# Gate scans in two pieces, and real products in the pauses before the first MLP pair, in an mLSTM and Fourier-mixing kernel

## The chip, the cores and the metric

The kernel runs on one core of one Trainium2 chip. A core has five engines that run at the same time and meet only at semaphores: TensorE (PE; the loading of its stationary operand is listed as PEld), VectorE (DVE), ScalarE (ACT), GpSimd (POOL) and SyncE (SP), which here issues the transfers. The metric is device time of one execution in microseconds (us); smaller is better.

## What is computed

Four sequences (batches) of 768 tokens pass through eight mLSTM heads of width 40, and the result, 320 wide, passes through a Fourier mix and an MLP. All is float32. Cut to what matters:

```python
# mLSTM, per batch, head and step t
m_new  = maximum(f_gate[t] + m, i_gate[t])
f_stab = exp(f_gate[t] + m - m_new);  i_stab = exp(i_gate[t] - m_new)
C = f_stab * C + i_stab * outer(v[t], k[t]);  n = f_stab * n + i_stab * k[t]
y[t] = sigmoid(o_gate[t]) * (C @ q[t]) / maximum(abs(n @ q[t]), 1)
# Fourier mix and MLP; x is (4, 768, 320), w_ch1 (320, 1280), w_ch2 (1280, 320)
u  = x + real(fft(fft(x, axis=seq), axis=feature))
un = (u - mean(u)) / sqrt(var(u) + 1e-6)
out = u + maximum(un @ w_ch1, 0) @ w_ch2
```

## The kernel before

The tokens are cut into six chunks of 128 (`NT = 6`, `L = 128`). Inside a chunk the recurrence is a masked product of scores and weights; between chunks a state `C` is carried. The running maximum `m` is a scan over tokens; all 32 (batch, head) rows are scanned at once in 32 partitions. Batches and chunks are counted from 0 below.

Every piece of work is entered in a plan by slot and phase, and the plan is emitted in order. Each engine then takes its own instructions strictly in the order in which they were emitted:

```python
EVAC, FILL, MAIN, FILL_PE = range(4)          # phases within a slot
def at(slot, phase, fn, *args): plan.setdefault((slot, phase), []).append((fn, args))
```

The gates come first. `sums` scans f within each chunk (F), `maxima` scans the running maximum M, `weights` makes wk = exp(a - M_last) on ACT, `decay` makes g on ACT, `columns` transposes rows to columns on PE. `parts` splits M into three bf16 parts on POOL, so that `spread_max` can spread a row of M over all partitions with a bf16 product; chunk 0 alone is spread in float32 from M itself, with a column of the identity:

```python
def spread_max(b, c, h0):
    ...
    k.M.append(bank("pM", [L, NP, L]))
    nc.tensor.matmul(k.M[-1], ident_b, later_b..., start=True, stop=False, ...)        # the mask
    for h in range(h0, h0 + NP):
        bh = b * H + h
        w, x = (ident[:, bh:bh + 1], M[:, c, :]) if c == 0 else (sel[:, bh:bh + 1], M3[:, c, :])
        nc.tensor.matmul(k.M[-1][:, h - h0, :], w.to_broadcast([w.shape[0], L]), x, ...)

first, second, others = slice(0, 1), slice(1, 2), slice(2, NT)
sums(first); maxima(first, M_INIT)
pt = columns(first, 0); nc.scalar.copy(out=colT[:, first, 0], in_=pt[:, first])
weights(first)
spread_max(0, 0, 0)
pt = columns(first, 1)
sums(second); maxima(second, M[0:BH, 0, L - 1:L]); parts(second)
columns_out(first, 1, pt)
pt = columns(second, 0)
spread_max(0, 0, NP)
mlstm_scores(0, 0); mlstm_exp(0, 0, 0); mlstm_exp(0, 0, NP)
mlstm_load_o(0, 1)
columns_out(second, 0, pt)
nc.vector.memset(g[:, 1:3], 0.0)
sums(others); maxima(others, M[0:BH, 1, L - 1:L])
decay(second); weights(second)
spread_max(0, 1, 0); spread_max(0, 1, NP); spread_decay(0, 1)
late = {1: columns(second, 1), 0: columns(others, 0)}
...
at(1, FILL + 0.2, parts, others)
at(2, FILL + 0.5, columns_late)            # DVE copies of late[1] and late[0]
at(4, FILL - 0.4, decay_late)              # g of the others (ACT), stored to G_d (SP)
at(5, FILL + 0.3, weights, others)         # wk of chunks 2 to 5 (ACT)
at(5, FILL_PE + 1.8, columns_last)         # their transposes (PE)
at(6, FILL - 0.2, ...)                     # and their copy to colT (DVE)
at(5, FILL_PE + 2.1, spread_decay, 0, 2)
for c in range(2, NT):
    for h0 in (0, NP): at(3 * c - 1, FILL_PE + 2, spread_max, 0, c, h0)
```

The plan of the mLSTM, for chunk c of batch b in slot s = s0 + 3 c (s0 is 0, 32, 50, 82 for the four batches), cut:

```python
if b > 0:
    t = 22 + 2 * c if b == 1 and c < 3 else s - 5
    at(t, FILL, mlstm_load, b, c); at(t, FILL, mlstm_load_max, b, c); at(t, FILL, mlstm_load_decay, b, c)
...
at(s - 1 if last else s, FILL_PE + (2.05 if last else 2), mlstm_scores, b, c)    # PE: k times q
at(s + 2, FILL, mlstm_weigh, b, c)          # DVE: scores times weights
at(s + 3, FILL_PE, mlstm_from_state, b, c)  # PE: C times q
at(s + 3, FILL_PE + 3, mlstm_from_chunk, b, c); at(s + 3, FILL_PE + 3, mlstm_to_state, b, c)
at(s + 4, FILL, mlstm_gather, b, c)         # ACT: out of PSUM, the state among it
```

(The first chunk of the first batch and the last one are placed apart.) The weights of the MLP come as 64-bit floats in ten pieces of 640 KB (`raw`) and are turned into float32 by DVE (`take`: L358, L360; `join`: L372, L374, L378) and ACT (`convert`: L365, L366), with two buffers for `raw`.

Where the first mix ends and the MLP begins (slots 22 to 31), PE has a few products of zeros in its plan, in slots 24, 25 and 26, each of 256 columns:

```python
def idle_products(n, first=False):
    pw = bank("pi", ...) if first else ps_s.tile([L, 2 * L], FP, name="pi", tag="ps")
    for i in range(n): nc.tensor.matmul(pw, rest[:, 0:L], rest, ...)
```

`mix_add` (DVE) adds the mix to x and takes the mean and variance of a chunk of tokens, `mix_center` (ACT) centers it, `mix_turn` (PE) transposes it, `mix_turn_out` (ACT) copies it to `uT`. The MLP of batch 0 takes three chunks of tokens at a time (a group; 384 columns), and two blocks of 128 hidden features at a time (a pair):

```python
def mlp_in(b, gr, f):
    if f % 2 == 0: k.pm = [bank("pm", [L, TG * L]) for _ in range(2)]
    for i, ch in ((1, 1),) if f % 2 else ((0, 0), (0, 1), (1, 0)):
        nc.tensor.matmul(k.pm[i], w1_sb[:, ch, ...], u[2 * ch], start=(ch == 0), stop=False)
    if f % 2:
        for i in range(2): nc.tensor.matmul(k.pm[i], w1t_sb[r, ...], u[1][r], start=False, stop=True)
```

PSUM has four banks for such use; the string `turn` says which bank each new tile takes.

Of the kernel before, what the change touches and what calls it, by code (L numbers as in the profile page):

```python
# [10 lines left out]
FP = mybir.dt.float32  # L11
# [8 lines left out]
L = 128  # L20
# [30 lines left out]
def kernel(  # L51
# [28 lines left out]
    ps_h = pool("ps_h", 2, space=PSUM)  # L80
    ps_m = pool("ps_m", 1, space=PSUM)

    turn = iter("3210321032120312031230123012012301023130201320132013201320123021320321")

    def bank(name, shape, n=None):

        return ps_m.tile(shape, FP, name=name, tag=f"pm{next(turn) if n is None else n}")
# [43 lines left out]
    EVAC, FILL, MAIN, FILL_PE = range(4)  # L131


    def idle_products(n, first=False):
        pw = bank("pi", [L, 2 * L]) if first else ps_s.tile([L, 2 * L], FP, name="pi", tag="ps")
        for i in range(n):
            nc.tensor.matmul(pw, rest[:, 0:L], rest, start=True, stop=True, skip_group_check=True)


    def gates(gp):  # L140
# [19 lines left out]
        idle_products(3, True)  # L160
        mlstm_load(0, 0)
        make_identity(nc, ident)
        nc.gpsimd.memset(later_b, 0.0)
# [5 lines left out]
        nc.vector.memset(keep, 1.0)  # L169
        nc.vector.memset(keep[:, :, 0:1], 0.0)  # L170
        nc.vector.memset(shift, 0.0)
        nc.vector.memset(M[:, 0:1], 0.0)
        for t in C_bufs:
            nc.scalar.copy(out=t.rearrange("p (two n) t -> p two (n t)", two=2),
                           in_=rest.unsqueeze(1).to_broadcast([L, 2, 2 * L]))
# [30 lines left out]
        def spread_max(b, c, h0):  # L206

            k = chunks[b, c]
            if h0 == 0:
                k.W = wp.tile([L, H, L], FP, name="W", tag="W")  # L210
                k.M = []
            k.M.append(bank("pM", [L, NP, L]))
            nc.tensor.matmul(k.M[-1], ident_b, later_b.unsqueeze(1).to_broadcast([L, NP, L]), start=True, stop=False,
                             skip_group_check=True)
            for h in range(h0, h0 + NP):
                bh = b * H + h
                w, x = (ident[:, bh:bh + 1], M[:, c, :]) if c == 0 else (sel[:, bh:bh + 1], M3[:, c, :])
# [31 lines left out]
                nc.tensor.transpose(pt[:, c, :], (a, wk)[j][:, c, :], ident[0:BH, 0:BH])  # L249
            return pt  # L250


        first, second, others = slice(0, 1), slice(1, 2), slice(2, NT)

        def columns_out(s, j, pt):
            nc.vector.tensor_copy(out=colT[:, s, j], in_=pt[:, s])

        sums(first)
        maxima(first, M_INIT)
        pt = columns(first, 0)  # L260
# [1 line left out]
        weights(first)  # L262
        spread_max(0, 0, 0)
        pt = columns(first, 1)
        sums(second)
        maxima(second, M[0:BH, 0, L - 1:L])
        parts(second)
        columns_out(first, 1, pt)
        pt = columns(second, 0)
        spread_max(0, 0, NP)  # L270
        mlstm_scores(0, 0)
        mlstm_exp(0, 0, 0)
        mlstm_exp(0, 0, NP)
        mlstm_load_o(0, 1)
        columns_out(second, 0, pt)
        nc.vector.memset(g[:, 1:3], 0.0)
        sums(others)
        maxima(others, M[0:BH, 1, L - 1:L])
        decay(second)
        weights(second)  # L280
        spread_max(0, 1, 0)
        spread_max(0, 1, NP)
        spread_decay(0, 1)
        late = {1: columns(second, 1), 0: columns(others, 0)}

        def clear(*tiles):
            for t in tiles:
                nc.gpsimd.memset(t, 0.0)

        def columns_late():  # L290
            columns_out(second, 1, late[1])
            columns_out(others, 0, late[0])

        def columns_last():
            late[2] = columns(others, 1)

        def decay_late():
            decay(others)
            for hip in range(2):
                nc.sync.dma_start(out=G_d[1:NT, hip].rearrange("c p t -> p c t"), in_=g[hip:BH:2, 1:NT])  # L300

# [13 lines left out]
            nc.sync.dma_start(out=M_d.rearrange("c p t -> p c t"), in_=M[0:BH])  # L315

        at(12, FILL + 0.7, maxima_out)
        at(1, FILL + 0.2, parts, others)
        at(5, FILL + 0.3, weights, others)
        at(5, FILL_PE + 1.8, columns_last)  # L320
        at(6, FILL - 0.2, lambda: columns_out(others, 1, late[2]))
        at(5, FILL_PE + 2.1, spread_decay, 0, 2)
        for c in range(2, NT):
            for h0 in (0, NP):
# [147 lines left out]
    def mlstm_scores(b, c):  # L472

        k = chunks[b, c]
        k.ps = [ps_s.tile([L, NP, L], FP, name=f"ps{hip}", tag="ps") for hip in range(2)]
        for p in range(NP):
            for hip in range(2):
                r = slice(hip * 64, hip * 64 + D)
                nc.tensor.matmul(k.ps[hip][:, p, :], k.qk[r, 1, p, :], k.qk[r, 0, p, :], start=True, stop=True)  # L479
# [87 lines left out]
    def plan_mlstm(b, s0, stride=3):  # L567
        for c in range(NT):
            s = s0 + stride * c
            if b > 0:  # L570
                t = 22 + 2 * c if b == 1 and c < 3 else s - 5
                at(t, FILL, mlstm_load, b, c)
                at(t, FILL, mlstm_load_max, b, c)
                at(t, FILL, mlstm_load_decay, b, c)
                at(s, FILL, mlstm_load_o, b, c)
            if (b, c) > (0, 0):
                at(s, FILL, mlstm_exp, b, c, 0)
                at(s + 1, FILL - 0.5, mlstm_exp, b, c, NP)
                last = (b, c) == (0, NT - 1)
                at(s - 1 if last else s, FILL_PE + (2.05 if last else 2), mlstm_scores, b, c)  # L580
                if b > 0:
                    at(s + 1, FILL, mlstm_mask, b, c)
            at(s, FILL, mlstm_scale_v, b, c)
            at(s if (b, c) == (0, 2) else s + 1, FILL + 0.1, mlstm_scale_q, b, c)
            at(s + 2, FILL, mlstm_decay, b, c)
            end = (b, c) == (0, NT - 1)
            at(s + 1 if end else s + 2, FILL - 0.4 if end else FILL, mlstm_weigh, b, c)
            at(s + 2 if end else s + 3, FILL_PE, mlstm_from_state, b, c)
            at(s + 2 if end else s + 3, FILL_PE + (2 if end else 3), mlstm_from_chunk, b, c)
            at(s + 3, FILL_PE + 3, mlstm_to_state, b, c)  # L590
            at(s + 3 if end else s + 4, FILL, mlstm_gather, b, c)
            if b == 0:
                t, x = ((8, 11), (11, 14), (13, 14), (14, 15.5), (17, 18), (18, 21))[c]
            else:
                t = s + (8, 8, 7, 5, 5, 5)[c]
                x = t + 1
            at(t, FILL_PE + ((2.5 if c < 4 else 1) if b == 0 else 1), mlstm_turn, b, c, b == 0 and c < 4)
            at(x, FILL + 0.05, mlstm_finish, b, c)
# [240 lines left out]
                at(t + 1, EVAC, mix_turn_out, b, c)  # L839


    def mlp_in(b, gr, f):


        k = mixes[b]
        u = [uT_bufs[gr][:, ch].rearrange("p c t -> p (c t)") for ch in range(3)]
        if f % 2 == 0:
            k.pm = [bank("pm", [L, TG * L]) for _ in range(2)]
        for i, ch in ((1, 1),) if f % 2 else ((0, 0), (0, 1), (1, 0)):
            f0 = (f // 2 * 2 + i) * L  # L850
            nc.tensor.matmul(k.pm[i], w1_sb[:, ch, f0:f0 + L], u[2 * ch], start=(ch == 0), stop=False)  # L851
        if f % 2:
            for i in range(2):
                r = slice(i * TAIL, (i + 1) * TAIL)
                nc.tensor.matmul(k.pm[i], w1t_sb[r, f // 2 * L:(f // 2 + 1) * L], u[1][r], start=False, stop=True)  # L855


    hid = {}
# [185 lines left out]
    def plan_mlp(b, s):  # L1044
# [7 lines left out]
                at(*((s, EVAC) if end else (s + n, MAIN + 0.5)), mlp_relu_in_place, gr, f)  # L1052
        for gr in groups if b == 0 else ():
            for f in range(NFF):
                at(s, MAIN, mlp_in, b, gr, f)
                s += 1
                if f % 2:
                    at(s, EVAC, mlp_relu, b, gr, f - 1)
                    at(s, EVAC, mlp_relu, b, gr, f)
# [24 lines left out]
    def plan_batch(b, s_mlstm, s_mix, s_mlp):  # L1084
# [161 lines left out]
```

## Time and profile before

| What | Value |
|---|---|
| time, median of 3 runs | 428.91 us (427.86 to 429.19) |
| span of the profiled execution | 427.5 us |
| mean granted PE clock, share of full speed | 0.984 |
| read from and written to device memory | 42.52 MB and 4.11 MB |
| `sums`, 128 and 512 columns (L191) | 0.41 and 1.15 us |
| scan of M, 128 and 512 columns (L199) | 0.47 and 1.27 us |
| one half of `spread_max`, float32, full clock (L213 and L218) | 0.39 and 1.09 us |
| one half of `spread_max`, bf16, full clock (L213 and L218) | 0.39 and 0.39 us |
| first `pu` product of the mix (L743) | starts at 58.85 us |

A line of the timeline gives start, length, engine, source line (L), operation, what is written and what is read, and in square brackets how long the engine had been idle before it and whom it waited for. A line of a group of waits gives engine, line and tile, then the one waited for, the total, the number of times and the longest. Float32 products appear as two matmul records each. Ends of matmuls are modelled, since PE works pipelined.

### The profile page before, as it was taken

The numbers are of one execution on the slowest core, as the hardware profiler recorded it, in microseconds if no ns is written. First come the engines' busy times: TensorE is split into PE (matmuls) and PEld (weight loads), VectorE is DVE, ScalarE is ACT, GpSimd is POOL, SyncE is SP. The second block draws the span as 40 slices with busy tenths as digits, with TensorE's granted clock in tenths as the row PEclk, the third lists the DMA queues.
The fourth block names the chain that finished last, engine by engine and source line by source line (L and its number), as shares of the span: only waits on it lengthen the run. The fifth ranks groups of instructions, "written<-read, shape, count | busy, mean of one in ns | idle before, by whom it ended". The sixth has DMA issues, their size and how long they took to land.

```text
span 427.5 us, 7999 instructions
## 1 busy us (share of the span) xinstructions
PE 412.9 (97%) x2958; PEld 305.4 (71%) x2958; DVE 289.0 (68%) x690; ACT 189.3 (44%) x493; POOL 116.8 (27%) x199
## 2 busy tenths in 40 slices
PE   8699899999999999999999999999999999999997
PEld 6478645566667777777557999977558988555996
DVE  7558886857997736687766487797754586335552
ACT  7637646767544411455546414464452023345000
POOL 7615501238642440433051152333030000020000
PEclk9669999999999999999999999999999999999999
DMA  7846849567763441546400343420000000000010
GB/s 233 272 138 166 301 124 283 191 215 208 224 200 115 159 145 44 158 144 189 141 0 1 95 151 117 139 65 2 0 2 0 32 31 18 15 0 2 15 45 33
DMA packets 20549, 47.14 MB, mean 110 GB/s; under 512 B 2784, under 2 KB 9312, under 8 KB 20384
## 3 DMA queue, kind: packets, MB, share of 16 engines
q1 hardware_dynamic: 20512, 46.65, 34.8%
q8 instruction: 23, 0.38, 0.4%
q14 instruction: 14, 0.11, 0.1%
HBM read 42.52 MB, written 4.11 MB: 109 GB/s over the span
## 4 chain that ended last, share of the span: by engine, by line
PE 83%; DVE 10%; ACT 3%; issue 2%; POOL 0%; ACTq 0%; DVEq 0%; POOLq 0%
PE po L1013 18%; PE pm L911 17%; PE po L957 8%; PE pm L916 5%; PE ph L500 5%; PE ps L479 5%; PE pm L851 5%; PE ph L493 4%; PE pu L743 3%; PE put L786 2%; PE px L549 2%; PE pz L712 2%; DVE W L485 1%; PE pm L855 1%; PE pz L700 1%
## 5 line engine op out<-in xcount | busy, mean ns | idle before, releaser
L963 DVE SCALAR_TENSOR_TENSOR x<-po,rstd,x 128x160 f32<-128x160 f32 (+1 forms) x69 | 27.0, 394 | 40.6 <-PE po L1013 34.2
L920 DVE TENSOR_TENSOR h<-h,pm 128x384 f32<-128x384 f32 x60 | 30.5, 550 | 30.5 <-ACT h L933 20.9
L435 ACT ACTIVATE W<-W,colT 128x128 f32<-128x128 f32 x144 | 45.0, 396 | 0.0
L457 POOL TENSOR_SCALAR_AFFINE_SELECT W<-W 128x1024 f32<-128x1024 f32 x18 | 21.5, 1195 | 79.8 <-ACT W L435 59.3
L957 PE MATMUL po<-w_sb,h 128*128 128x320 f32 x120 | 34.4, 435 | 0.0
L485 DVE TENSOR_TENSOR W<-ps,W 128x512 f32<-128x512 f32 x48 | 30.7, 679 | 4.7 <-POOL W L457 4.5
L911 PE MATMUL pm<-uT,w_sb 128*128 128x384 f32 x90 | 32.8, 492 | 0.2 <-DVE uT L899 0.2
L851 PE MATMUL pm<-uT,w_sb 128*128 128x384 f32 x80 | 29.8, 500 | 0.7 <-DVE x L763 0.5
L479 PE MATMUL ps<-qk 40*128 40x128 f32 x384 | 28.4, 285 | 0.8 <-DVE W L485 0.6
L957 PEld LDWEIGHTS po<-w_sb,h 128*128 128x128 f32 x120 | 22.2, 190 | 9.5 <-issue 0.8
L791 ACT COPY uT<-put 128x384 f32<-128x384 f32 x24 | 11.2, 478 | 40.2 <-PE put L786 40.2
L1013 PE MATMUL po<-T,S 128*128 128x160 f32 x180 | 27.9, 302 | 0.6 <-DVE x L963 0.6
L479 PEld LDWEIGHTS ps<-qk 40*128 40x128 f32 x384 | 23.8, 188 | 5.3 <-DVE W L485 1.1
L806 POOL TENSOR_TENSOR t<-rstd 128x6 f32<-128x6 f32 x12 | 3.1, 256 | 89.2 <-DVE v L804 88.6
L1013 PEld LDWEIGHTS po<-T,S 128*128 128x128 f32 x180 | 25.5, 190 | 2.2 <-DVE x L963 1.0
L500 PE MATMUL ph<-W,kvt 128*41 128x128 f32 x384 | 26.7, 282 | 0.0
L1013 PE MATMUL po<-w_sb,h 128*128 128x160 f32 x180 | 26.4, 301 | 0.0
L1013 PEld LDWEIGHTS po<-w_sb,h 128*128 128x128 f32 x180 | 25.1, 190 | 1.3 <-DVE x L963 0.3
L493 PEld LDWEIGHTS ph<-qg,C 128*128 128x128 f32 x160 | 20.8, 198 | 6.4 <-issue 2.1
L538 ACT COPY h<-ph 41x512 f32<-41x512 f32 (+1 forms) x16 | 9.3, 583 | 35.6 <-PE ph L500 35.5
L445 POOL TENSOR_TENSOR qg<-qk,Gb 128x512 f32<-128x512 f32 x18 | 25.0, 1390 | 0.1
L493 PE MATMUL ph<-qg,C 128*128 128x128 f32 x160 | 22.7, 286 | 1.6 <-POOL eo L632 0.8
(205 smaller groups left out, 868.5 us busy)
## 6 DMA issues: line engine op xcount, KB each, us to landing
W<-M_d SPq DMA_DIRECT2D x18, 512.0 KB
kvt<-in_kv SPq DMA_DIRECT2D x24, 324.0 KB
qk<-in_qkT SPq DMA_DIRECT2D x48, 160.0 KB
raw<-in_w SPq DMA_DIRECT2D x10, 640.0 KB
Gb<-G_d SPq DMA_DIRECT2D x36, 128.0 KB
so<-in_o SPq DMA_DIRECT2D x24, 160.0 KB
out<-x SPq DMA_DIRECT2D x24, 160.0 KB
ds_sb<-in_dft_s SPq DMA_DIRECT2D x1, 1155.0 KB
```

The source lines that it names most:

```text
L435: nc.scalar.activation(out=k.W[:, h, :], in_=M, func=AF.Exp, scale=-1.0, bias=colT[:, c, 0, b * H + h:b * H + h + 1])
L445: nc.gpsimd.tensor_tensor(out=k.qg, in0=k.qk[:, 0], in1=k.Gb, op=OP.mult)
L479: nc.tensor.matmul(k.ps[hip][:, p, :], k.qk[r, 1, p, :], k.qk[r, 0, p, :], start=True, stop=True)
L485: nc.vector.tensor_tensor(out=Wv, in0=k.ps[hip], in1=Wv, op=OP.mult)
L493: nc.tensor.matmul(k.ph[:, p, :], k.C[:, p, :], k.qg[:, p, :], start=(p == 0), stop=False, skip_group_check=True)
L500: nc.tensor.matmul(k.ph[hip * 64:hip * 64 + D1, p, :], k.v1[:, 2 * p + hip, :], k.W[:, 2 * p + hip, :], start=(c == 0 and p == 0), stop=Tr ...
L851: nc.tensor.matmul(k.pm[i], w1_sb[:, ch, f0:f0 + L], u[2 * ch], start=(ch == 0), stop=False)
L911: nc.tensor.matmul(bank, w, u, start=start, stop=True, skip_group_check=True)
L920: nc.vector.tensor_tensor(out=h, in0=h, in1=bank, op=OP.add)
L957: nc.tensor.matmul(k.po, hidden(gr, f)[:, i * L:(i + 1) * L], w2_sb[:, f, :], start=(f == 0), stop=(f == NFF - 1))
L963: nc.vector.scalar_tensor_tensor(out=u, in0=po, scalar=k.rstd[:, c:c + 1], in1=u, op0=OP.mult, op1=OP.add)
L1013: nc.tensor.matmul(po, a[:, f], w[:, f], start=start and f == 0, stop=f == half - 1, skip_group_check=True)
```

## The change

The gates of chunk 1 are no longer scanned by themselves: chunk 0 is scanned alone, and chunks 1 to 5 in one scan each of F and M. The maxima of chunk 1 are spread in float32 from M, as those of chunk 0, instead of from three bf16 parts; the split on POOL covers chunks 2 to 5. The wk of chunks 1 to 5 are made and transposed together, before the scores of chunk 1, where wk of chunks 2 to 5 had come in slot 5.

The zero products of slots 24 to 26 go. In their place stand the scores of the first chunk of batch 1, in two halves, and the part of the first MLP pair that covers the first two chunks of tokens (256 columns); the third chunk of tokens (128 columns) follows in slot 31. For that, the loads of the first three chunks of batch 1 come in slots 18, 20 and 22 instead of 22, 24 and 26. The `mix_add` of the fourth chunk of tokens comes in slot 27 instead of 31, and the order of PSUM banks is fitted to it.

```diff
-    turn = iter("3210321032120312031230123012012301023130201320132013201320123021320321")
+    turn = iter("3210321032120312031230123010122301023130201320132013201320123021320321")
...
-        nc.vector.memset(M[:, 0:1], 0.0)
+        nc.vector.memset(M[:, 0:2], 0.0)
...
-                w, x = (ident[:, bh:bh + 1], M[:, c, :]) if c == 0 else (sel[:, bh:bh + 1], M3[:, c, :])
+                w, x = (ident[:, bh:bh + 1], M[:, c, :]) if c < 2 else (sel[:, bh:bh + 1], M3[:, c, :])
...
-        first, second, others = slice(0, 1), slice(1, 2), slice(2, NT)
+        first, others, last = slice(0, 1), slice(1, NT), slice(2, NT)
...
         spread_max(0, 0, 0)
         pt = columns(first, 1)
-        sums(second)
-        maxima(second, M[0:BH, 0, L - 1:L])
-        parts(second)
-        columns_out(first, 1, pt)
-        pt = columns(second, 0)
         spread_max(0, 0, NP)
         mlstm_scores(0, 0)
+        sums(others)
         mlstm_exp(0, 0, 0)
+        nc.vector.tensor_copy(out=colT[:, first, 1], in_=pt[:, first])
         mlstm_exp(0, 0, NP)
+        maxima(others, M[0:BH, 0, L - 1:L])
+        pt = columns(others, 0)
         mlstm_load_o(0, 1)
-        columns_out(second, 0, pt)
         nc.vector.memset(g[:, 1:3], 0.0)
-        sums(others)
-        maxima(others, M[0:BH, 1, L - 1:L])
-        decay(second)
-        weights(second)
+        nc.vector.tensor_copy(out=colT[:, others, 0], in_=pt[:, others])
+        decay(slice(1, 2))
+        weights(others)
         spread_max(0, 1, 0)
         spread_max(0, 1, NP)
         spread_decay(0, 1)
-        late = {1: columns(second, 1), 0: columns(others, 0)}
+        pt = columns(others, 1)
+        late = {"pt": pt}
...
-            decay(others)
+            decay(last)
...
-        at(1, FILL + 0.2, parts, others)
-        at(5, FILL + 0.3, weights, others)
-        at(5, FILL_PE + 1.8, columns_last)
-        at(6, FILL - 0.2, lambda: columns_out(others, 1, late[2]))
+        at(1, FILL + 0.2, parts, last)
...
-                t = 22 + 2 * c if b == 1 and c < 3 else s - 5
+                t = 18 + 2 * c if b == 1 and c < 3 else s - 5
...
-                at(s - 1 if last else s, FILL_PE + (2.05 if last else 2), mlstm_scores, b, c)
+                if (b, c) == (1, 0):
+                    at(24, FILL_PE + 5.5, mlstm_scores, b, c, (0, NP // 2))
+                    at(25, FILL_PE + 5.5, mlstm_scores, b, c, (NP // 2, NP))
+                else:
+                    at(s - 1 if last else s, FILL_PE + (2.05 if last else 2), mlstm_scores, b, c)
...
-                at(s, MAIN, mlp_in, b, gr, f)
+                two = (0, 2 * L)
+                if gr == 0 and f == 0:
+                    at(26, FILL_PE + 4.5, mlp_in, b, gr, f, two, (0, 1))
+                    at(26, FILL_PE + 5.5, mlp_in, b, gr, f, two, (1, 3))
+                    at(26, FILL_PE + 5.5, mlp_in, b, gr, f + 1, two)
+                at(s, MAIN, mlp_in, b, gr, f, (2 * L, TG * L) if gr == 0 and f < 2 else (0, TG * L))
...
-            add = turn + [s_mlp, s_mlp + 4, s_mlp + 6]
+            add = turn + [s_mlp - 4, s_mlp + 4, s_mlp + 6]
...
-    for s, phase, n in ((24, 5.5, 1), (25, 5.5, 1), (26, 5.5, 1)):
-        at(s, FILL_PE + phase, idle_products, n)
```

`mlp_in` and `mlstm_scores` take the range of columns, or of head pairs, as new arguments. What is computed stays the same.

More of the change, by code (lines that the diff above doesn't have):

```diff
@@ L131, with idle_products @@
     EVAC, FILL, MAIN, FILL_PE = range(4)
-    def idle_products(n, first=False):
-        pw = bank("pi", [L, 2 * L]) if first else ps_s.tile([L, 2 * L], FP, name="pi", tag="ps")
+    def idle_products(n):
+        pw = bank("pi", [L, 2 * L])
         for i in range(n):
@@ L159, in gates @@
         nc.scalar.activation(out=warm, in_=rest[:, 0:1], func=AF.Exp)
-        idle_products(3, True)
+        idle_products(3)
         mlstm_load(0, 0)
@@ L250, in columns @@
             return pt
-        first, second, others = slice(0, 1), slice(1, 2), slice(2, NT)
-        def columns_out(s, j, pt):
-            nc.vector.tensor_copy(out=colT[:, s, j], in_=pt[:, s])
+        first, others, last = slice(0, 1), slice(1, NT), slice(2, NT)
         sums(first)
@@ L290, in columns_late @@
         def columns_late():
[L291 to L295, printed above, removed]
+            nc.vector.tensor_copy(out=colT[:, others, 1], in_=late["pt"][:, others])
         def decay_late():
-            decay(others)
+            decay(last)
             for hip in range(2):
@@ L470, in mlstm_decay, with mlstm_scores @@
                                         op=OP.mult)
-    def mlstm_scores(b, c):
+    def mlstm_scores(b, c, pairs=(0, NP)):
         k = chunks[b, c]
-        k.ps = [ps_s.tile([L, NP, L], FP, name=f"ps{hip}", tag="ps") for hip in range(2)]
-        for p in range(NP):
+        if pairs[0] == 0:
+            k.ps = [ps_s.tile([L, NP, L], FP, name=f"ps{hip}", tag="ps") for hip in range(2)]
+        for p in range(*pairs):
             for hip in range(2):
@@ L839, in plan_mix, with mlp_in @@
                 at(t + 1, EVAC, mix_turn_out, b, c)
-    def mlp_in(b, gr, f):
+    def mlp_in(b, gr, f, t=(0, TG * L), which=(0, 3)):
         k = mixes[b]
-        u = [uT_bufs[gr][:, ch].rearrange("p c t -> p (c t)") for ch in range(3)]
-        if f % 2 == 0:
+        t = slice(*t)
+        u = [uT_bufs[gr][:, ch].rearrange("p c t -> p (c t)")[:, t] for ch in range(3)]
+        if f % 2 == 0 and t.start == which[0] == 0:
             k.pm = [bank("pm", [L, TG * L]) for _ in range(2)]
-        for i, ch in ((1, 1),) if f % 2 else ((0, 0), (0, 1), (1, 0)):
+        for i, ch in ((1, 1),) if f % 2 else ((0, 0), (0, 1), (1, 0))[slice(*which)]:
             f0 = (f // 2 * 2 + i) * L
-            nc.tensor.matmul(k.pm[i], w1_sb[:, ch, f0:f0 + L], u[2 * ch], start=(ch == 0), stop=False)
+            nc.tensor.matmul(k.pm[i][:, t], w1_sb[:, ch, f0:f0 + L], u[2 * ch], start=(ch == t.start == 0), stop=False,
+                             skip_group_check=True)
         if f % 2:
@@ L854, in mlp_in @@
                 r = slice(i * TAIL, (i + 1) * TAIL)
-                nc.tensor.matmul(k.pm[i], w1t_sb[r, f // 2 * L:(f // 2 + 1) * L], u[1][r], start=False, stop=True)
+                nc.tensor.matmul(k.pm[i][:, t], w1t_sb[r, f // 2 * L:(f // 2 + 1) * L], u[1][r], start=False, stop=True,
+                                 skip_group_check=True)
     hid = {}
```

## The prediction

> **What bounds the kernel now.** I read the page first: busy shares and the clock row. Columns of the first row: busy microseconds, share of the span, instructions.
>
> ```profile
> PE 412.9 (97%) x2958; PEld 305.4 (71%) x2958; DVE 289.0 (68%) x690; ACT 189.3 (44%) x493; POOL 116.8 (27%) x199
> ...
> PEclk9669999999999999999999999999999999999999
> ```
>
> TensorE (PE) is busy 97% of 427.5 us, so only three things can pay: less PE work, fewer PE gaps, or a faster PE clock. The clock row has two slices at 6, the second and third of 10.7 us each. So I asked for engine time by stretch (columns: stretch, length, busy of PE, PEld, DVE, ACT, POOL with counts, granted clock, DMA share, GB/s).
>
> ```profile
> 8.00:12.00 4.00, 3.98 (x51) 3.10 (x50) 3.90 (x7) 3.52 (x14) 2.47 (x3) 1.00 1.02 340
> 12.00:16.00 4.00, 3.27 (x32) 2.85 (x34) 3.06 (x8) 1.39 (x6) 3.77 (x4) 0.78 0.99 337
> 16.00:20.00 4.00, 1.42 (x22) 1.11 (x17) 1.44 (x3) 3.11 (x7) 2.52 (x5) 0.50 0.77 253
> 20.00:24.00 4.00, 3.21 (x17) 2.04 (x18) 0.29 (x1) 2.63 (x10) 1.03 (x4) 0.50 0.48 157
> 24.00:28.00 4.00, 4.00 (x28) 3.45 (x28) 2.16 (x3) 1.16 (x5) 0.00 (x0) 0.51 0.08 23
> ```
>
> The clock is halved from about 14.4 to 27.5 us, and in the middle PE hardly works. Who it waits for is in the waits of PE over the whole run (total, times, longest):
>
> ```profile
> PE pt L249 <- ACT wk L240: 3.4, 1, 3.4
> PE put L786 <- ACT uc L779: 1.3, 4, 0.4
> PE ph L493 <- POOL eo L632: 0.8, 1, 0.8
> ```
>
> The largest PE wait of the kernel is a gate matter: transposes of `wk`, which ScalarE (ACT) computes late. Its timeline shows why (start, length, idle before):
>
> ```profile
> 16.83 0.60 ACT L525 COPY C<-pc 40x164 f32<-40x164 f32 x2 [3.43 <-PE pc L510]
> 17.44 1.17 ACT L538 COPY h<-ph 41x512 f32<-41x512 f32 x2
> 18.64 0.47 ACT L543 ACTIVATE so<-so 128x320 f32<-128x320 f32 x1
> 19.01 0.81 ACT L365 ACTIVATE e<-e,ebias 128x640 uint32<-128x640 uint32 x1
> 19.73 0.72 ACT L366 ACTIVATE m<-m 128x640 f32<-128x640 uint32 x1
> 20.36 1.26 ACT L240 ACTIVATE wk<-a,nM 32x128 f32<-32x128 f32 x4
> ```
>
> ACT idles 3.43 us, then does 3.5 us of other work, and only then the four `wk` that PE needs. From 66 us on PE has under 1% of idle time until the last stores, so a shift of the front should reach the end. The second place touched is the gap before the first MLP pair (PE timeline):
>
> ```profile
> 64.21 0.60 PE L137 MATMUL pi<-rest 128*128 128x256 f32 x2
> 65.01 0.55 PE L786 MATMUL put<-ident,uc 128*128 128x128 f32 x3 [0.20 <-ACT uc L779]
> 65.40 0.60 PE L137 MATMUL pi<-rest 128*128 128x256 f32 x2
> 66.13 2.85 PE L851 MATMUL pm<-uT,w_sb 128*128 128x384 f32 x8
> 68.91 0.92 PE L855 MATMUL pm<-uT,w1t_sb 64*128 64x384 f32 x4
> 69.65 1.06 PE L479 MATMUL ps<-qk 40*128 40x128 f32 x16
> ```
>
> Zero products (`pi`) fill the pauses, and the real work comes behind.
>
> **What the Trainium skill says.** "TensorE: Matmul & The Clock Gate", Part 1: the PE clock is at half rate when idle and rises after about 3.4 us of sustained work, in free-running windows. The trace agrees: 16 passes of L500 take 1.93 us at 14.30 and 1.07 at 28.84. The same page, queue depths: ScalarE and VectorE are strict FIFO; hence `wk` stuck behind work that itself waited for PE. "SBUF — State Buffer", Who interferes with whom: VectorE (DVE) and GpSimd (POOL) share a port pair, held for a whole instruction. The trace agrees: the copy of `shift` (L198) takes 0.13 us at 5.06 but 0.69 at 9.28, ending 9.97 as POOL's L451 ends (9.95).
>
> **The change part by part: gates.** Up to 4.49 us nothing changes. Sizes in between I interpolate from 128 and 512 columns: F scan 0.41 and 1.15 us, 640 columns 1.40; subtraction 0.28 and 0.73, so 0.88; M scan 0.47 and 1.27, so 1.54. DVE: F scan 4.42 to 5.8, then it waits for the transposed `wk` of chunk 0 (PE, 6.92), copies it (7.1), subtracts (8.0), `shift` copy (8.2), M scan (9.8), `nM` and `m_in` (10.4), memset of `g` (10.7), copy of `a` columns (11.0), weighs chunk 0, 1.28 us, to 12.3 (before: 13.17).
>
> PE: scores of chunk 0 end at about 9.46, five transposes 0.5 (9.95). Maxima of chunk 1 are now f32 products with the identity: per half 0.39 (L213) and 1.09 (L218, eight passes), where bf16 parts took 0.39 and 0.39. Two halves: 2.96 against 1.56, a **cost of 1.4 us**; ends 12.9. Decay of chunk 1, 1.09: 14.0. ACT has by then done one `g` and all five `wk` (6 x 0.32, from 10.75 to 12.7), so their transposes follow at once: 14.5. Scores of chunk 1 1.16 (15.7), products of chunk 0 1.07 (16.7), state 0.4: 17.1. Before, the same point was 16.80: a **draw**.
>
> Then the gain. PE needs `pd` 0.36, spread of chunk 2's maxima 2 x 0.77, decay 1.09, from-state 1.06, scores 1.16, from-chunk 1.00, state 0.6: 6.8 us, to 23.9. Inputs: the split of M (POOL, 5.4 us from 9.8) ends at 15.2; chunk 1's exponentials 12.7 to 15.0; the late `g` 16.3. All are earlier than their use. Before, this point was 30.52 (the last L515). **Gain 6.6 us**: the wait of 3.4, its transposes of 1.2 in that place, and about 2 of half clock; the clock stays up since PE has no pause from 7 to 24 us.
>
> From there to 47 us the kernel is set by DVE in order: joins, takes, weighing, finishes (3.86, 3.79, 3.72 of 4 us busy from 36 to 48). The first join begins when ACT's conversion is done: 20.8 instead of 26.4, and the second would end near 29 instead of 36.4. So the lead carries at 6 to 7 us.
>
> **Gap before the MLP.** Before, PE's second `pu` group ends near 62.25 and pair plus scores at 70.71: 8.46 us. The work in it: three turns 1.0, scores 1.05, pair 3.7. Split, two thirds of the pair (2.46) go ahead; the last third has 12 passes of 128 columns at 0.134 (as L218), 1.6, so **0.4 dearer** than a third of 3.7. Sum 6.1; waits left for `uc` and `uT` (0.46, 0.2, 0.5) 1.2. End at 62.25 + 7.3 = 69.55: gain 1.1, and I take 0.9 since the third turn now stands behind a product that waits for the second `uT`.
>
> **Loads and residual.** The loads of chunks 1 and 2 of batch 1 (all counted from 0) were issued at 58.64 and 61.91, behind a weight load that waits for its buffer; they go ahead of it, to where DMA is at 0.09 to 0.20 (52 to 60 us). That empties 60 to 76 us (share 0.89 to 1.05), where DVE waited 5.2 us for `raw`; PE worked through that, so I count 0 to 0.3. The fourth `mix_add` (1.15 us of DVE) only moves.
>
> Sum: -6.6 - 0.9 = -7.5, 421.4. I give back 0.6 for DVE and POOL colliding in the longer gate block and for waits that return between 28 and 50 us: **422.0 us**.
>
> **Rivals.** (1) *The clock stays low*: if windows between 10 and 17 us count the narrow products (40 rows, 32 columns) as idle, half clock costs about 3 of the 6.6: 425. For it: before, the clock fell after a stretch with PE only about three quarters busy. Against: from 48 to 52 us it is 3.00 of 4 busy and keeps 1.00, and the new stretch is fuller. (2) *The gate block becomes the bound*: chunk 1 now waits for the long scan and f32 spread; if the M scan slips by a microsecond or two (POOL's L451 beside it), all PE work behind slips, and the separate scan was worth having: 427 to 430. For it: PE arrives at 9.95, just as M is ready, so every slip counts. Against: the `wk` wait is gone in any case. (3) *DVE or DMA takes the lead back*: from 28 to 48 us DVE is nearly full and DMA is at 0.5 to 1.0; if raw weights or tables land no sooner, the front arrives early and waits: 425 to 428. For it: L709 starts at 52.07 just as heavy DMA traffic ends. Against: those transfers are issued when buffers come free, and these come free earlier too.
>
> **Range and chances.** About 0.65 for the whole lead (420.5 to 422.5), 0.25 for a part (423 to 427), 0.1 for none. Eight in ten: 419.0 to 427.5. Faster by over 2% means under 420.3, 8.6 us: all of the lead and the gap at their best, 0.20. Slower by over 2% needs a fault I don't see, 0.02. The rest, 0.78, lies within 2%.
>
> **What would show it.** Right: no wait of `pt` for `wk`; clock 1.00 from 7 to 28 us; the state of chunk 1 (last L515 of the first group) at 24 instead of 30.5; the first fold of the mix at about 40.5 instead of 47.3; L218 of chunk 1 in f32 ending near 12.9; the third part of the first pair directly followed by the second pair, about 7.3 us after `pu`. Wrong: clock at 0.5 beyond 14 us (rival 1), PE waiting for M or `g` between 9 and 14 (rival 2), DVE waiting for `raw` or PE for tables between 28 and 46 (rival 3); or a lead at 47 us which is gone by 130.

## The result, and the profile after

The changed kernel takes 423.34 us (median of 4 runs, 423.03 to 424.96), against 428.5 us of the kernel before measured beside it (427.86 to 429.19). The ratio is 0.9887, with a 95% interval of 0.9855 to 0.9919: **faster by 1.1%**. The predicted time was 422.0 us, the predicted gain 6.9 us; measured are 5.2 us. That lies in the range foretold for "a part" of the lead (423 to 427 us), not in that for the whole lead (420.5 to 422.5).

On the page of the changed kernel, TensorE has 4.5 us less to do, as the model of the profile counts busy time, and the clock row has no dip left:

```profile
PE 408.4 (97%) x2972; PEld 303.5 (72%) x2972; DVE 289.3 (69%) x682; ACT 189.2 (45%) x493; POOL 112.6 (27%) x194
...
PEclk9999999999999999999999999999999999999999
```

PE has 14 matmul records more than before and is still busy for less time, mainly because a matmul at half clock is listed about twice as long. Engine time by stretch, same columns as before, and one stretch further on:

```profile
12.00:16.00 4.00, 4.00 (x58) 3.55 (x59) 2.52 (x5) 4.00 (x16) 3.56 (x5) 1.00 1.02 335
16.00:20.00 4.00, 3.58 (x55) 2.86 (x52) 2.82 (x7) 3.73 (x9) 1.33 (x4) 1.00 0.61 193
20.00:24.00 4.00, 4.00 (x67) 3.27 (x66) 3.93 (x7) 3.10 (x12) 1.08 (x5) 1.00 0.63 206
24.00:28.00 4.00, 3.60 (x47) 3.19 (x46) 3.16 (x4) 4.00 (x13) 2.71 (x5) 1.00 0.88 270
64.00:68.00 4.00, 2.64 (x12) 1.00 (x10) 2.43 (x5) 3.36 (x9) 1.80 (x2) 1.00 0.88 276
```

From 12 to 28 us the clock is 1.00 and PE is busy about 90% or more, where before it had 1.42 of 4 us between 16 and 20. The last line is new trouble: between 64 and 68 us PE has work for 2.64 of 4 us. The waits of PE name it:

```profile
PE put L778 <- ACT uc L771: 2.4, 4, 1.4
PE ph L480 <- DVE den L545: 1.4, 1, 1.4
```

The wait for `wk` is gone. In its place there are two of 1.4 us, where the longest of these kinds were 0.4 and 0.6 us before. (Line numbers moved: `put` was L786, from-state L493, the weight conversion L358.)

The timeline of ACT shows `wk` in its new place, five at once, and ahead of the exponentials of chunk 1:

```profile
11.43 0.40 ACT L244 ACTIVATE g<-M,m_in 32x128 f32<-32x128 f32 x1 [1.75 <-DVE g L269]
11.74 1.55 ACT L240 ACTIVATE wk<-a,nM 32x128 f32<-32x128 f32 x5
...
13.20 2.09 ACT L421 ACTIVATE W<-pM,colT 128x128 f32<-128x128 f32 x8
```

And the timeline of PE at the first MLP pair, in four lines: products of 256 columns (the first two chunks of tokens), then of 128 (the third), then the second pair, then a transpose that PE waited 1.36 us for:

```profile
60.39 0.70 PE L849 MATMUL pm<-uT,w1t_sb 64*128 64x256 f32 x4
61.02 1.16 PE L844 MATMUL pm<-uT,w_sb 128*128 128x128 f32 x8
62.11 0.49 PE L849 MATMUL pm<-uT,w1t_sb 64*128 64x128 f32 x4
62.53 2.20 PE L844 MATMUL pm<-uT,w_sb 128*128 128x384 f32 x6
...
66.09 0.55 PE L778 MATMUL put<-ident,uc 128*128 128x128 f32 x3 [1.36 <-ACT uc L771]
```

In the kernel before, the same transpose did not wait:

```profile
72.68 0.49 PE L786 MATMUL put<-ident,uc 128*128 128x128 f32 x3
```

The centering that it needs starts 6.35 us sooner than before, while the second pair starts 8.11 us sooner. These are the two lines of ACT, first before, then changed:

```profile
71.78 0.61 ACT L779 ACTIVATE uc<-x 128x384 f32<-128x384 f32 x1
65.43 0.61 ACT L771 ACTIVATE uc<-x 128x384 f32<-128x384 f32 x1
```

**Where the time came from and went.** PE runs the same products in both kernels, so the start of one and the same product in both traces gives the lead at that place. All numbers are starts in us on PE, read from the timelines; the lead over the kernel before is in brackets. The profiled run of the kernel before has a mean clock of 0.984, and most of its runs (49 of the 65 timed beside the experiments) have 0.991 or 0.992; so the leads are larger than against a usual run, but not their differences behind the front. The last two columns are experiments told below.

| Place | before | changed | gates alone | centering sooner |
|---|---|---|---|---|
| from-chunk of chunk 1, batch 0 | 28.84 | 21.60 (7.24) | 21.15 (7.69) | 20.88 (7.96) |
| first `pu` of the mix | 58.85 | 51.61 (7.24) | 51.16 (7.69) | 50.89 (7.96) |
| second MLP pair | 70.64 | 62.53 (8.11) | 62.96 (7.68) | 61.81 (8.83) |
| third `pu` of the mix | 74.60 | 68.06 (6.54) | 66.91 (7.69) | 66.30 (8.30) |
| from-chunk of chunk 0, batch 1 | 80.51 | 73.75 (6.76) | 72.90 (7.61) | 71.99 (8.52) |
| from-chunk of chunk 4, batch 1 | 120.64 | 115.05 (5.59) | 113.04 (7.60) | 112.02 (8.62) |
| span | 427.5 | 421.9 (5.6) | 419.9 (7.6) | 418.9 (8.6) |

The gates make a lead of 7.24 us by 22 us of time, and it stands until the mix. The split pair adds 0.87. Then **2.5 us are lost** at two places: 1.57 between the second pair and the third `pu`, and 1.17 between chunks 0 and 4 of batch 1 (0.22 comes back between the two). From there to the end the lead does not move.

The second loss is seen in DVE's timeline:

```profile
98.67 0.91 DVE L344 TENSOR_SCALAR e<-raw 128x640 uint32<-128x640 uint32 x1 [2.71 <-DMA raw<-in_w]
...
101.09 1.29 DVE L472 TENSOR_TENSOR W<-ps,W 128x512 f32<-128x512 f32 x2
...
108.97 0.50 DVE L344 TENSOR_SCALAR e<-raw 128x640 uint32<-128x640 uint32 x1 [1.34 <-DMA raw<-in_w]
```

DVE stands 2.71 and then 1.34 us before raw weights that have not landed. The weighing of chunks 3 and 4 (L472), which PE needs, is behind that in DVE's order. Before, the same two steps waited 0.65 us and not at all. The lead falls by 0.40 at chunk 3 and by 0.77 at chunk 4, where PE's wait for `den`, behind the weighing in DVE's order, is 1.42 us instead of 0.64:

```profile
112.90 1.13 PE L480 MATMUL ph<-qg,C 128*128 128x128 f32 x8 [1.42 <-DVE den L545]
```

### The profile page after: what moved, and what is told of

It is laid out like the page before. It is cut to its first block, busy times and chain, and to the rows that moved or that the text cites. A ratio compares the mean times of both kernels' runs of the same rounds, so it can differ in the third digit from the quotient of the medians.

```text
span 421.9 us, 8010 instructions
## 1 busy us (share of the span) xinstructions
PE 408.4 (97%) x2972; PEld 303.5 (72%) x2972; DVE 289.3 (69%) x682; ACT 189.2 (45%) x493; POOL 112.6 (27%) x194
## 4 chain that ended last, share of the span: by engine, by line
PE 77%; DVE 10%; issue 3%; DMA 3%; ACT 3%; POOL 2%; ACTq 0%; DVEq 0%; POOLq 0%
PE po L1008 18%; PE pm L906 17%; PE po L952 8%; PE pm L911 5%; PE ph L487 4%; PE ps L466 4%; PE pu L735 4%; PE ph L480 3%; DMA raw<-in_w 3%; PE px L536 2%; PE put L778 2%; PE pz L704 2%; PE pm L844 2%; DVE W L472 1%; PE pz L692 1%
## 5 line engine op out<-in xcount | busy, mean ns | idle before, releaser
L472 DVE TENSOR_TENSOR W<-ps,W 128x512 f32<-128x512 f32 x48 | 30.7, 680 | 4.1 <-POOL W L443 3.9
L906 PE MATMUL pm<-uT,w_sb 128*128 128x384 f32 x90 | 32.8, 492 | 0.2 <-DVE uT L894 0.2
L844 PE MATMUL pm<-uT,w_sb 128*128 128x384 f32 (+2 forms) x88 | 30.1, 470 | 0.9 <-DVE x L755 0.5
L487 PE MATMUL ph<-W,kvt 128*41 128x128 f32 x384 | 25.8, 277 | 0.0
L906 PEld LDWEIGHTS pm<-uT,w_sb 128*128 128x128 f32 x90 | 16.2, 190 | 10.9 <-DVE h L915 1.5
```

Source lines behind the costliest of these rows:

```text
L472: nc.vector.tensor_tensor(out=Wv, in0=k.ps[hip], in1=Wv, op=OP.mult)
L487: nc.tensor.matmul(k.ph[hip * 64:hip * 64 + D1, p, :], k.v1[:, 2 * p + hip, :], k.W[:, 2 * p + hip, :], start=(c == 0 and p == 0), stop=Tr ...
L844: nc.tensor.matmul(k.pm[i][:, t], w1_sb[:, ch, f0:f0 + L], u[2 * ch], start=(ch == t.start == 0), stop=False, skip_group_check=True)
L906: nc.tensor.matmul(bank, w, u, start=start, stop=True, skip_group_check=True)
```

## The experiments

Each was timed beside the kernel before on one chip; ratios are to that, with 95% intervals. Not all were on the same chip, so medians of different groups are not compared to less than a microsecond, and the lead at the places of the table is used instead. The first four are one group, on one chip.

**Gates alone.** The kernel before with the gate hunks of the change and nothing else of it:

```diff
+        first, others, last = slice(0, 1), slice(1, NT), slice(2, NT)
 ... all other gate lines of the change
```

> The kernel before with the gates of the change alone; zero products, loads and the fourth mix_add as before. If the gates make the whole lead (theory A): first pu product of the mix at 51.6 us instead of 58.9, lead 7.2 us there. Then two ways. A1, the stretch from 60 to 118 us takes lead back whatever stands before the MLP (weights that land no sooner): end at 422.5 to 424.0 us, with VectorE waiting 2 us or more for raw. A2, the other parts of the change spoil it: end at 421.0 to 421.6 us, the full 7.2 kept. Rival B, the gates make only part of the lead: mix later than 53 us.

Measured: 421.88 us (421.62 to 422.14), ratio 0.9855 (0.9831 to 0.988). The table has its leads: 7.69 us at the mix, 7.6 at the end. **A2 holds, and A1 falls**: the gates' lead survives the whole stretch if the rest of the change is absent. (The time is 0.3 us above the range of A2.) B falls too. In its stretches the hole is not there (same columns as above):

```profile
64.00:68.00 4.00, 4.00 (x17) 2.19 (x16) 0.00 (x0) 1.18 (x3) 1.80 (x2) 1.00 1.03 311
```

**The rest alone.** The changed kernel with the gates of before:

```diff
-        first, others, last = slice(0, 1), slice(1, NT), slice(2, NT)
+        first, second, others = slice(0, 1), slice(1, 2), slice(2, NT)
 ... all other gate lines as before
```

> The changed kernel with the gates of before: products in the pauses, sooner loads, sooner fourth mix_add. Theory A: mix at 58.9 us as before, second pair starts about 0.9 us sooner than 70.6, but TensorE then waits about 1.4 us for uc of the fourth chunk of tokens, so that at the first chunk of batch 1 the lead is -0.5 to +0.2 us, and the time is 428.0 to 429.0 us. Rival: the part is worth its 0.9 us to the end, 427.3 to 427.8 us.

Measured: 428.4 us (427.11 to 431.59), ratio 1.0005 (0.9989 to 1.0021): **nothing gained**. The front of the profiled run is 1.36 us ahead with the same gates: 0.29 by 14 us, the rest while the clock was at half in the profiled run of the kernel before (for 13.7 us in all, against 6.8 here). So I take differences of leads: second pair +0.87 (68.41 against 70.64), chunk 0 of batch 1 -0.48 net, chunk 4 of batch 1 -1.68 net. Both losses appear without the new gates, with the same wait of 1.36 us for `uc`, and again DVE waits for the last two raw weights (0.90 and 1.54 us). Theory A's numbers were met; it had named the first loss only.

**wk sooner.** The kernel before, with its separate scan of chunk 1, and one line changed:

```diff
-        at(5, FILL + 0.3, weights, others)
+        at(4, FILL - 0.3, weights, others)
```

> The kernel before, with one edit: ScalarE makes wk of chunks 2 to 5 in slot 4 beside the late g, ahead of the copies out of PSUM, instead of in slot 5; chunk 1 is still scanned by itself. If the order of wk is what cost the time (and not the separate scan): no wait of pt for wk, 3.4 us less there, and with the clock kept up 5.5 to 7.5 us of lead at the mix, end at 421.5 to 424 us. If the clock still falls at 14.4 us: lead 3 to 4.5 us, end at 424.5 to 426 us. If the separate scan is the cost: lead under 2 us, end above 426.5 us.

Measured: 423.44 us median, ratio 0.9879 (0.9831 to 0.9927), and two groups that the mean granted clock tells apart: 420.21, 421.19, 421.31 at clock 0.999 to 1.000, and 425.57, 425.89, 426.15 at 0.988. So the order of `wk` was the cost, **not the separate scan**; with the clock up, this one line gives as much as all the gate hunks. The profiled run is of the second group; its lead at the mix is 3.72 us. The page's clock row and PE's timeline show how it loses:

```profile
PEclk9689999999999999999999999999999999999999
```

```profile
11.21 0.41 PE L249 MATMUL pt<-ident,a 32*128 32x32 f32 x4
12.52 2.52 PE L479 MATMUL ps<-qk 40*128 40x128 f32 x16 [0.90 <-DVE W L485]
14.97 1.93 PE L500 MATMUL ph<-W,kvt 128*41 128x128 f32 x16
```

The clock fell at 13.3 us, while the scores of chunk 1 ran, and stayed at half for 10.2 us. Ahead of that stand small transposes and one pause of 0.90 us. The scores take 2.52 us instead of 1.16; not all of that is the clock, for in the kernel before they took 1.75 us behind a like pause while the clock was still at 1.00.

**The wait filled.** The kernel before; the wait stays, zero products go into it:

```diff
+        at(5, FILL_PE + 1.7, fill_wait)    # three zero products, 256 columns each, in a free bank
         at(5, FILL_PE + 1.8, columns_last)
```

> The kernel before, with three zero products of 256 columns (about 2.9 us at half clock) put into TensorE's wait for wk. The wait stays; only the clock can change. If the half clock after the wait is a cost of its own: clock back at 1.00 by about 21 us instead of 27.5, work of 6.7 us there in about 3.7, lead of 2 to 3 us at the mix, end at 425.5 to 427 us. If the wait alone matters, because the work after it is set by other engines: mix at 58.5 to 59, end at 428.3 to 429 us.

Measured: 427.86 us, ratio 0.9981 (0.996 to 1.0001), **inconclusive as a remedy**. By clock the 22 runs part again: at 1.00, 424.1 to 425.78 (4 runs); at 0.995 and 0.996, 426.61 and 426.73; at 0.991 and 0.992, 427.05 to 428.75 (14 runs); two are at 0.987 and 0.98. None of the 65 runs of the kernel before is above 0.992, so the products seem to help the clock in some runs. A clock that stays up is worth some 2.5 us here (medians 425.4 and 428.0). In the profiled run (0.996, lead 2.30 us at chunk 1) the clock had fallen at 13.7 us and was back at 17.1, ahead of the three products, which began at 17.58 and took 1.56 us; 2.15 us of wait were left, and the clock stayed at 1.00 through them. So this run does not show whether the products can bring the clock back.

The next four, on another chip, are the changed kernel: three with one edit each, and one with two of these edits.

**Centering sooner.** `mix_add` of the fourth chunk of tokens had moved to slot 27; its centering had stayed in slot 33, behind eight exponentials on ACT:

```diff
-            at(t, FILL + 0.1, mix_center, b, c)
+            at(28 if (b, c) == (0, ORDER[3]) else t, FILL + 0.1, mix_center, b, c)
```

> The changed kernel, with the centering (ScalarE) of the fourth chunk of tokens in slot 28 instead of 33, ahead of the exponentials of batch 1; its transpose stays. If the pause before that transpose is what ate the gain of the split pair: TensorE's wait for uc falls from 1.4 us to under 0.3, the third pu product of the mix comes at 66.7 to 67.2 instead of 68.1, and the end gains 0.8 to 1.3 us, 421.9 to 422.5 us. Rival: VectorE, held up by late raw weights, takes the gain back by chunk 4 of batch 1: end unchanged, 423.0 to 423.8 us.

Measured: 420.52 us (419.5 to 421.51), ratio 0.9825 (0.9801 to 0.9849). The transpose no longer waits for `uc` (what it still waits for is 0.32 us of another thing):

```profile
61.81 2.20 PE L844 MATMUL pm<-uT,w_sb 128*128 128x384 f32 x6
64.33 0.55 PE L778 MATMUL put<-ident,uc 128*128 128x128 f32 x3 [0.32 <-ACT h L859]
```

From the first `pu` to chunk 0 of batch 1 the lead rises by 0.56 instead of falling by 0.48: **the pause cost 1.0 us**, as expected. The time is at least 1.4 us better than expected; part of that is that the second loss is absent here as well (8.52 to 8.62; DVE's waits for those raw weights were 1.1 and 0), and in the profiled run the front is 0.72 us further ahead. The rival, a gain lost again to raw weights, falls.

**Takes later.** The first step of the last two weight conversions goes behind the weighing:

```diff
+    when[8] = ((43, 0.1), (43, 0.7), (44, 0.6))
+    when[9] = ((46, 0.1), (46, 0.7), (47, 0.6))
```

> The changed kernel, with the first step of the conversion of the last two weight pieces (VectorE, waits for raw) placed behind the weighing of chunks 3 and 4 of batch 1 instead of ahead of it. If the second loss (lead 6.8 to 5.6 us between 94 and 115 us) is VectorE standing in order before raw weights that have not landed: lead of 6.5 us or more at chunk 4 of batch 1, end at 421.9 to 422.6 us. Rival: the loss comes from the work and port of VectorE itself: end unchanged, 423.0 to 423.8 us, or the conversion now delays the next chunk.

Measured: 422.46 us (420.33 to 425.65), ratio 0.9883 (0.9848 to 0.9918), which cannot be told from the change itself. The trace can: the lead now rises from chunk 0 to chunk 4 of batch 1 (7.92 to 8.87) where it fell from 6.76 to 5.59. DVE weighs first and finds the raw weights there:

```profile
98.12 1.29 DVE L472 TENSOR_TENSOR W<-ps,W 128x512 f32<-128x512 f32 x2 [3.30 <-POOL W L443]
99.33 0.77 DVE L344 TENSOR_SCALAR e<-raw 128x640 uint32<-128x640 uint32 x1
```

PE's wait for `den` is gone too. So the mechanism is shown in the trace, and its worth in time is not shown by this run alone.

**Loads back.**

```diff
-                t = 18 + 2 * c if b == 1 and c < 3 else s - 5
+                t = 22 + 2 * c if b == 1 and c < 3 else s - 5
```

> The changed kernel, with the loads of chunks 0 to 2 of batch 1 back in slots 22, 24, 26. If their new place is what makes the last raw weights land late: raw waits of VectorE after 90 us fall from 4.0 to 1.5 us or less and the end gains about 1 us (422.0 to 422.6); VectorE waits 5 us for raw near 68 us again, at no cost. Rival: the place of these loads does not matter to the end, 423.0 to 423.8 us.

Measured: 421.8 us (420.67 to 422.72), ratio 0.9852 (0.9829 to 0.9876). Raw waits after 90 us are 1.1 and 0.4 us, DVE waits 4.65 us near 69 us at no cost, and the lead falls by 0.15 instead of 1.17 between chunks 0 and 4. That is what the theory asked for, but the last group takes it back.

**Both edits** (centering sooner, takes later):

> The changed kernel with both edits, centering of the fourth chunk of tokens sooner and the last two takes later. If each loss is a wait of its own, the gains add: end at 420.8 to 421.7 us, at or below the kernel with the gates alone (421.9). If one hides the other: 422 to 422.8 us.

Measured: 419.28 us median (418.65 to 419.39, and one of 424.91 at clock 0.992), ratio **0.9813** (0.977 to 0.9856). Leads: 8.59 at the mix, 9.21 at chunk 0 of batch 1, 10.16 at chunk 4 and to the end. The time is below both expectations; neither loss is left, and the gains add, so the losses are waits of their own.

The last group, on another chip:

**The change again**, no edit:

> The changed kernel itself once more, so that its edits can be compared on one chip with more runs. If the median on record stands: 423.0 to 423.8 us, clock 0.996 to 1.00 in every run, lead at the mix 7 to 8.5 us depending on when the gates land.

Measured: 423.4 us (421.43 to 426.02), ratio 0.9896 (0.9857 to 0.9936). The lead goes 7.92 at the mix, 7.45 at chunk 0, 7.12 at chunk 4: the first loss is as before, the second 0.3 instead of 1.2. DVE waited 1.3 and 0.4 us for the raw weights. So the second loss differs from execution to execution. One thing was not as expected: one run (426.02 us) had a clock of 0.992.

**Both edits, loads back:** the two edits above and that of the loads.

> The changed kernel with centering sooner and the last two takes later, and the loads of chunks 0 to 2 of batch 1 back in slots 22, 24, 26. If the sooner loads are a cost of their own (one experiment had 421.8 with them back): 0.5 us or more under the kernel with both edits, 418.3 to 418.8 us. If they only mattered through the late raw weights, which the later takes already hide: same, 419.0 to 419.6 us.

Measured: 421.01 us (419.95 to 424.8), ratio 0.9841 (0.9803 to 0.9878). **Not better than with the sooner loads**, rather worse, and neither expectation holds. At the mix the lead is that of "both edits" (8.63 against 8.59), but at chunk 0 of batch 1 it is 8.27 against 9.21. In between, DVE, ACT and PE have a new chain of waits:

```profile
67.89 0.49 DVE L344 TENSOR_SCALAR e<-raw 128x640 uint32<-128x640 uint32 x1 [5.01 <-DMA raw<-in_w]
69.78 0.85 ACT L859 ACTIVATE h<-pm 128x384 f32<-128x384 f32 x2
70.30 0.30 PEld L844 LDWEIGHTS pm<-uT,w_sb 128*128 128x128 f32 x2 [1.81 <-ACT h L859]
70.30 0.91 PE L844 MATMUL pm<-uT,w_sb 128*128 128x384 f32 x2 [1.19 <-DMA qk<-in_qkT]
```

PE stands 1.19 us before a product of the MLP. The profile puts PE's wait down to a load of `qk`, which this product does not read; the loading of its weights waited for the relu on ACT (L859), whose first half ends at about 70.25. That fits better. The relu stands behind the conversion of weights for which DVE had waited 5.01 us. "Gates alone" and "loads back" have that wait of DVE as well (5.31 and 4.65 us), at little or no cost: their leads fall by 0.08 and not at all between the third `pu` and chunk 0 of batch 1. So in these two traces the sooner loads are worth about 0.9 us behind "centering sooner". The scores in the pauses did not wait for their loads: they start at 54.6 us here and in "both edits". Whether the sooner loads also delay the last raw weights stays open.

**wk sooner, clock held.** As "wk sooner", with two zero products in the pause of 0.9 us:

```diff
+        at(3, FILL_PE + 1.9, keep_clock)    # two zero products, 256 columns each
```

> The kernel before with wk of chunks 2 to 5 in slot 4 (as in the experiment that had two groups of times, 420.2 to 421.3 at clock 0.999 or more and 425.6 to 426.2 at 0.988), and two zero products of 256 columns in TensorE's pause of 0.9 us ahead of the scores of chunk 1. If the half clock makes the two groups: clock 0.996 or more in nearly all runs, one group, 420.3 to 421.6 us. If something else does: two groups again, or 425 to 426 us.

Measured: 421.46 us (420.99 to 423.32), ratio 0.9847 (0.9818 to 0.9875). Clock 0.999 or 1.000 in all six runs, and the group at 425.6 to 426.2 is gone: the half clock had made it. The second loss appears here too (lead 8.95 at chunk 0 of batch 1, 8.22 at chunk 4, DVE's waits for raw weights 1.06 and 1.19 us), though this kernel has none of the lines of the change. So neither the sooner loads nor the products in the pauses are needed for it.

**All of it, with the separate scan.** These gates, the rest of the change, and both edits:

> Chunk 1 scanned by itself with wk sooner and the two zero products, and behind it everything of the change but its gates, with centering sooner and the last two takes later. If the two gate blocks differ only in the clock that they risk: the same as the kernel with both edits, 418.7 to 419.6 us. If the separate scan saves what the bf16 parts are cheaper (1.4 us): 417.5 to 418.5 us.

Measured: 419.16 us (418.51 to 422.15), ratio **0.98** (0.9767 to 0.9833), the same as with both edits. The two gate blocks are worth the same once `wk` is early and the clock is held; the 1.4 us that float32 spreading costs do not show at the end. This and "both edits" are the fastest kernels here, each below the change.

## Why the prediction was right, and which term was mis-sized

**Gates: right in mechanism and size.** Foretold were -6.6 us, against the profiled run of the kernel before; against that run the traces measure -7.24 (the change) and -7.69 (gates alone). By medians the gates alone are worth -6.5 (421.88 against 428.34), since a usual run of the kernel before has less half clock than the profiled one. `wk`, the clock, and the draw at chunk 0 came as worked out: the second float32 spread ended at 12.75 us (12.9 in the working), the last L502 of chunk 1 at 23.26 (23.9), the first fold of the mix began at 40.11 (40.5). The leads differ from run to run in part because of the start: in the changed kernel's profiled run DVE waited 0.75 us for the input gates, which in "both edits" it did not.

One collision was missed. The working gave the copy of `shift` 0.2 us; beside POOL's L437 it took 0.69 (8.17 to 8.86; L437 ended at 8.84). The copies of 0.13 and 0.69 us that the prediction compared are not of one size (1 and 4 columns). That it waits for POOL shows better in its ends: in "wk sooner, clock held" a copy of 4 columns took 0.25 us and ended at 8.52, as POOL's L227 ended at 8.50.

**Clock: right.** The working took 2 to 3 us for it. "The wait filled" has 2.5 us between the runs at 1.00 and those at 0.991 and 0.992; in "wk sooner" it is 4.7 us between the groups (421.2 and 425.9, medians). Rival 1 came true in part: of the ten runs of the change seven are at 1.00, and three (0.992, 0.995 and 0.996) took 424.9 to 426.0 us, near the 425 that it named. Where the clock fell in these three no trace shows.

**Gap before the MLP: the term that was mis-sized.** I wrote "gain 1.1, and I take 0.9", counted to the start of the second pair, and that far it holds: 0.87. I then carried it to the end because "PE has under 1% of idle time". That idle share belonged to a PE which had the scores, about 1.0 us, between the pairs. With the scores gone ahead, PE came to the transpose of the fourth chunk sooner than ACT could serve it (1.36 us of wait): its order there is conversion, four exponentials, relu, four exponentials, centering. The term measures -0.87 and +1.35 (0.48 net loss by chunk 0 of batch 1), where I had -0.9. What the working left out is this wait for `uc` of the fourth chunk, 1.36 us where it had none. "Centering sooner" shows it by turning the loss into a gain of 0.56.

**Loads and residual: sign wrong.** I counted 0 to 0.3 us of gain. Between 94 and 115 us, 0.3 to 1.2 us were lost in the two profiled runs of the change, through DVE standing in order before the last raw weights. That is rival 3's mechanism, at a place where I did not look: I had put it between 28 and 48 us. What makes these weights land later is not settled; the loss also stands in "wk sooner, clock held", which has the loads in their old place. That the sooner loads gain nothing held for the change itself, but behind "centering sooner" they are worth about 0.9 us. "Only moves" was right of the fourth `mix_add` itself, and was the trouble: its successor on ACT had not moved with it.

Sum in the profiled runs: -7.24 - 0.87 + 1.35 + 1.17 = -5.59, and the spans differ by 427.5 - 421.9 = 5.6. That the total came within 1.4 us of 422.0 is partly luck: in these traces the gates give 0.6 us more than foretold, and the 0.6 us set aside for collisions was not used up, against 2.5 us lost behind them.

## What to carry to other kernels

When work is moved forward into the pauses of the busiest engine, look where that engine arrives next: it gets there sooner, and the producer that used to be in time stands in a queue that did not move. Move the whole chain (add, center, transpose), not its first link, and put steps that wait for a transfer behind those that the critical engine waits for. And if one line of emission order causes the largest wait, try that line alone first: with the clock held up, it gave here what a rearranged gate block gave.

## What the runs showed of the hardware that was not expected

The PE clock fell to half after less than a long pause. In "wk sooner" one pause of 0.90 us, with small transposes ahead of it, stands ahead of the fall (at 13.3 us), and three of six runs have the lower mean clock; two zero products (1.13 us of work) in the pause prevented it in six of six. Even in the kernel before, the clock fell at 14.2 us, behind a pause of 0.64 us and ahead of the wait of 3.37 us for `wk`. The Trainium skill ("TensorE: Matmul & The Clock Gate", Part 1) gives an idle window of about 3.4 us as the condition in its table of states; no idle time of that length stands ahead of these falls, so the measurement decides. A rule does not follow from these runs: in "the rest alone" the same pause of 0.90 us left the clock at 1.00 until 19.7 us, in the wait for `wk`, and the changed kernel kept 1.00 between 64 and 68 us with PE busy for 2.64 of 4 us.

What does agree is the length. In four traces the clock stayed at half for 13.65 us (the kernel before, 14.24 to 27.90), 10.24 ("wk sooner", 13.30 to 23.54), 6.83 ("the rest alone", 19.74 to 26.56) and 3.41 ("the wait filled", 13.72 to 17.14): four, three, two and one times 3.41 us. One such stretch is 0.004 of the mean clock (3.41 us at half, of 427), and the mean clocks of the kernel before do gather at 0.992, 0.988 and 0.984.

The landing of one and the same 640 KB weight piece, from issue to the DVE step that waited for it, took 4.8 us before (98.63 to 103.39) and 6.8 us in the changed kernel (91.86 to 98.67), with the same loads issued around it in the same order. Nothing in these runs explains the difference.
